# Two attention reads and a max-out layer: a bridge in DRAM, or one pass over the batches

## The chip, the cores and the metric

The kernel runs on one core of one Trainium2 chip. The metric is the device time of one execution in microseconds, taken as the median of several runs. A profile of one execution stands beside it; its clock runs from the first to the last instruction (the span). TensorE is PE in the profile, with its weight loads as PEld; VectorE is DVE, ScalarE is ACT, GpSimd is POOL, and SyncE, which only issues DMAs here, is SP.

## The reference

Eight batches, each with 8 heads, 512 tokens, 32 state rows and 64 values per head. Tokens read from the state and the state reads from the tokens; both results, 544 rows of 512 values per batch, go through a layer that takes the larger of two products.

```python
scores = scale * np.matmul(x, state.transpose(0, 1, 3, 2))
...
xread = np.matmul(a, state)
scores2 = scale * np.matmul(state, x.transpose(0, 1, 3, 2))
...
sread = np.matmul(a2, x)
return np.concatenate([xread, sread], axis=2).astype(np.float32)
...
h1 = x @ w1
h2 = x @ w2
g = np.maximum(h1, h2)
return (g @ w_out).astype(np.float32)
```

Here `a` and `a2` are softmaxes of the two score arrays. w1 and w2 are 512 x 1024, w_out is 1024 x 512, all in float32, as are x, state and the output of 4,352 rows (8 x 544).

## The kernel before, in words

Two stages stand one after the other, and a DRAM tensor `bridge` (512 x 4352, bf16) lies between them.

The attention stage loops over 8 batches and 8 heads. Per batch GpSimd's queue loads x and state with a cast to bf16 (L52, L57); x comes with tokens on partitions. Per head the kernel transposes the head's state (L61) and x (four transposes, L67) on TensorE, ScalarE copies them out of PSUM, four matmuls make the scores (L74), ScalarE takes the exponential (L78), VectorE sums, inverts and multiplies (L80, L83, L85). The normalised weights are transposed (L89), copied by ScalarE (L92) and multiplied by the state (L95, one matmul of 512 columns). VectorE casts the result (L97) and SP writes it to the bridge. The state's own read uses the same exponentials as weights (L106) and sums them with a column of ones (L108); the sums are turned by a transpose (L113), inverted (L117) and applied (L121), the result is transposed (L124) and written to the bridge too. Each kind of PSUM tile has one buffer, `p1` to `p8`. The order of the instructions of neighbouring heads is found by the framework's scheduler.

The MoE stage loads w1, w2 and w_out on GpSimd's queue (L144 to L148). Its tiles lie in memory that the first stage gives free, so that its first load waits for the last bridge write. Then it goes over 34 tiles of 128 rows: a load from the bridge (L155), eight slices of 128 hidden values with four matmuls for h1 (L164) and four for h2 (L167), a ScalarE cast of h1 to SBUF (L169) and a VectorE max with h2 (L170), then eight matmuls of 512 columns with w_out (L173), a VectorE copy (L176) and the store.

## Time and profile before

| What | us |
|---|---|
| Median of 3 runs | 427.98 (427.73 to 428.76) |
| Profiled execution, its span | 426.0 |
| TensorE busy | 376.9 (88%) |
| VectorE busy | 212.5 (50%) |
| ScalarE busy | 187.4 (44%) |
| GpSimd busy | 21.3 (5%) |
| Moved by DMA | 26.11 MB, mean 61 GB/s |

The profiled execution has no other time of its own than the span, which lies 2.0 us below the median of the runs. To read it: the busy shares are means over the two stages; the table by stage, the chain of waits and the timeline say which engine a stage waits for. Matmuls are pipelined, so the distance between the starts of two matmuls is their price, and the duration of one is longer.

### The profile page before, as it was taken

The numbers are of one execution on the slowest core, as the hardware profiler recorded it, in microseconds if no ns is written. First come the engines' busy times: TensorE is split into PE (matmuls) and PEld (weight loads), VectorE is DVE, ScalarE is ACT, GpSimd is POOL, SyncE is SP. The second block draws the span as 40 slices with busy tenths as digits, with TensorE's granted clock in tenths as the row PEclk, the third lists the DMA queues.
The fourth block names the chain that finished last, engine by engine and source line by source line (L and its number), as shares of the span: only waits on it lengthen the run. The fifth ranks groups of instructions, "written<-read, shape, count | busy, mean of one in ns | idle before, by whom it ended". The sixth has DMA issues, their size and how long they took to land.

```text
span 426.0 us, 10657 instructions
## 1 busy us (share of the span) xinstructions
PE 376.9 (88%) x3950; PEld 263.0 (62%) x3984; DVE 212.5 (50%) x755; ACT 187.4 (44%) x721; POOL 21.3 (5%) x25
## 2 busy tenths in 40 slices
PE   1999989999999999999860699999999999999996
PEld 1555555555455555555430578888888888888884
DVE  0455555554555545554540145555555555555553
ACT  1655555555555555555530233433433334333331
POOL 4002010020100201000002000000000000000000
PEclk9999999999999999999999999999999999999999
DMA  9209209091090911801016912222222222222211
GB/s 93 25 22 74 63 22 74 22 73 27 22 73 21 74 26 24 72 22 25 20 22 118 195 64 77 75 76 76 75 76 75 75 76 78 76 76 76 75 63 51
DMA packets 70307, 26.11 MB, mean 61 GB/s; under 512 B 59760, under 2 KB 64880, under 8 KB 70256
## 3 DMA queue, kind: packets, MB, share of 16 engines
q0 software_dynamic: 37168, 7.60, 20.7%
q1 hardware_dynamic: 33088, 17.84, 14.9%
q8 instruction: 31, 0.51, 0.5%
q14 instruction: 20, 0.16, 0.1%
HBM read 19.66 MB, written 13.37 MB: 78 GB/s over the span
## 4 chain that ended last, share of the span: by engine, by line
PE 79%; ACT 8%; DMA 6%; DVE 3%; issue 2%; POOL 0%; ACTq 0%; POOLq 0%; DVEq 0%
PE ph L167 14%; PE ph L164 14%; PE po L173 13%; PE p_xT L67 10%; PE p_xr L95 9%; ACT aT L92 8%; PE p_aT L89 8%; PE p_sr L106 5%; DMA wo<-in_moe_w_out_dram 4%; PE p_rs L113 2%; PE p_sT L61 2%; DMA x_bf<-in_x_dram 2%; PE p_rs L108 2%; DVE sr L121 1%; DMA bridge<-xr 0%
## 5 line engine op out<-in xcount | busy, mean ns | idle before, releaser
L169 ACT CAST gT<-ph 128x128 bf16<-128x128 f32 x272 | 72.3, 266 | 126.1 <-PE ph L164 126.0
L164 PE MATMUL ph<-xt,w 128*128 128x128 bf16 x1088 | 105.8, 221 | 12.2 <-DMA w<-in_moe_w_dram 12.1
L167 PE MATMUL ph<-xt,w 128*128 128x128 bf16 x1088 | 104.0, 219 | 1.8 <-DMA w<-in_moe_w_dram 1.8
L170 DVE TENSOR_TENSOR gT<-gT,ph 128x128 bf16<-128x128 bf16 x272 | 77.5, 287 | 52.9 <-ACT gT L169 31.5
L164 PEld LDWEIGHTS <-w 128*128 128x128 bf16 x1088 | 74.5, 99 | 21.4 <-issue 13.5
L167 PEld LDWEIGHTS <-w 128*128 128x128 bf16 x1088 | 72.7, 98 | 2.9 <-DMA w<-in_moe_w_dram 2.1
L67 PE MATMUL p_xT<-ident_bf,x_bf 128*64 128x128 bf16 x256 | 53.3, 315 | 9.3 <-DMA x_bf<-in_x_dram 8.7
L173 PE MATMUL po<-wo,gT 128*128 128x512 bf16 x238 | 57.1, 379 | 3.2 <-DMA wo<-in_moe_w_out_dram 1.5
L80 DVE TENSOR_REDUCE esum<-e_bf 128x4 f32<-128x128 bf16 x64 | 18.3, 285 | 80.0 <-ACT e_bf L78 80.0
L95 PE MATMUL p_xr<-aT,s_bf 32*64 32x512 bf16 x64 | 37.4, 584 | 13.2 <-ACT aT L92 13.2
L97 DVE CAST xr<-p_xr 64x512 bf16<-64x512 f32 x64 | 43.7, 683 | 9.9 <-PE p_xr L95 4.5
L176 DVE COPY ob<-po 128x512 f32<-128x512 f32 x34 | 23.5, 692 | 48.4 <-PE po L173 48.4
L106 PEld LDWEIGHTS <-e_bf 128*32 128x32 bf16 x256 | 21.8, 122 | 41.4 <-ACT e_bf L78 41.4
L92 ACT COPY aT<-p_aT 32x512 bf16<-32x512 bf16 x64 | 36.8, 575 | 23.6 <-PE p_aT L89 23.6
L173 PEld LDWEIGHTS <-gT 128*128 128x128 bf16 x272 | 25.2, 98 | 25.8 <-issue 1.6
L70 ACT COPY xT<-p_xT 64x512 bf16<-64x512 bf16 x64 | 36.2, 565 | 8.1 <-PE p_xT L67 8.0
L89 PE MATMUL p_aT<-ident_bf,a_bf 128*32 128x128 bf16 x256 | 38.9, 307 | 0.5 <-DVE a_bf L85 0.4
L67 PEld LDWEIGHTS <-x_bf 128*64 128x64 bf16 x256 | 23.7, 142 | 15.4 <-DMA x_bf<-in_x_dram 8.7
L63 ACT COPY sT<-p_sT 64x32 bf16<-64x32 bf16 x64 | 11.4, 179 | 44.4 <-PE p_sT L61 44.4
L106 PE MATMUL p_sr<-x_bf,e_bf 128*32 128x64 bf16 x256 | 30.4, 220 | 0.5 <-ACT e_bf L78 0.4
L108 PE MATMUL p_rs<-e_bf,ones_bf 128*1 128x32 bf16 x256 | 29.0, 213 | 0.0
L74 PE MATMUL p_sc<-sT,xT 64*128 64x32 bf16 x256 | 28.9, 193 | 0.0
(32 smaller groups left out, 269.9 us busy)
## 6 DMA issues: line engine op xcount, KB each, us to landing
out_dram<-ob SPq DMA_DIRECT2D x34, 256.0 KB, 2.0
xt<-bridge SPq DMA_DIRECT2D x34, 128.0 KB, 2.3
x_bf<-in_x_dram POOLq DMA_DIRECT2D x8, 512.0 KB, 7.7
bridge<-xr SPq DMA_DIRECT2D x64, 64.0 KB, 1.9
w<-in_moe_w_dram POOLq DMA_DIRECT2D x2, 1024.0 KB, 10.5
bridge<-srT SPq DMA_DIRECT2D x64, 4.0 KB, 1.6
wo<-in_moe_w_out_dram POOLq DMA_DIRECT2D x1, 1024.0 KB, 17.1
s_bf<-in_state_dram POOLq DMA_DIRECT2D x8, 32.0 KB, 5.3
```

The lines of the kernel that those rows point to most:

```text
L67: nc.tensor.matmul(p_xT[:, c, :], x_bf[:, h, c, :], ident_bf, is_transpose=True, start=(c == 0), stop=(c == NC - 1))
L89: nc.tensor.matmul(p_aT[:, c, :], a_bf[:, c, :], ident_bf, is_transpose=True, start=(c == 0), stop=(c == NC - 1))
L92: nc.scalar.copy(aT, p_aT)
L95: nc.tensor.matmul(p_xr, s_bf[:, h, :], aT.rearrange("n c p -> n (c p)"))
L97: nc.vector.tensor_copy(xr, p_xr)
L106: nc.tensor.matmul(p_sr, e_bf[:, c, :], x_bf[:, h, c, :], start=(c == 0), stop=(c == NC - 1))
L108: nc.tensor.matmul(p_rs, ones_bf, e_bf[:, c, :], start=(c == 0), stop=(c == NC - 1))
L164: nc.tensor.matmul(ph1[:, :mt], w1[:, k, f * 128:(f + 1) * 128], xt[:, k, :mt], start=(k == 0), stop=(k == n_k - 1))
L167: nc.tensor.matmul(ph2[:, :mt], w2[:, k, f * 128:(f + 1) * 128], xt[:, k, :mt], start=(k == 0), stop=(k == n_k - 1))
L169: nc.scalar.copy(gT[:, f, :mt], ph1[:, :mt])
L170: nc.vector.tensor_max(gT[:, f, :mt], gT[:, f, :mt], ph2[:, :mt])
L173: nc.tensor.matmul(po[:mt, :], gT[:, f, :mt], wo[:, f, :], start=(f == 0), stop=(f == n_kf - 1))
```

## The change

The kernel becomes one pass over the batches, and the bridge goes.

- Weights are combined on the chip. `wcat` holds Wc = w1 - w2 (1024 columns) and W2 Wo (512 columns). As max(h1, h2) = h2 + relu(h1 - h2), the output is relu(x (w1 - w2)) w_out + x (W2 Wo).
- The read of the state is folded into the layer. The 8 heads' state rows of a batch, multiplied by their part of `wcat`, make `SW` (2 x 128 pairs of head and state row, 1536 columns; `u_sw`, in three chunks of 512 columns, each eight matmuls of 64 x 32 weights). Layer 1 multiplies the attention weights `A` (transposed, `AT`) by `SW`.
- Attention works on all heads of a batch at once: x is loaded as float32 with 1 KB pieces, cast by GpSimd (batch 0 by VectorE and ScalarE), transposed 128 x 128; scores go against a block-diagonal state `sbd`; the sums for the state's read come from a column of ones in `xb`. GpSimd multiplies A by the inverse sums.
- The state's reads of all batches are kept in `sread_t` and pass the layer together in `moe_sread`, after batch 5.
- The order is written out by hand (`manual_schedule`). Three batches of attention (LEAD) run ahead, with the transposes of w2 (`w_t`) behind the first and W2 Wo (`w_wo`) behind the third. Then `moe(b)` has slots, after each of its eight layer-1 slices and four layer-2 tiles, filled with the attention of batch b+3 and `u_sw` of batch b+1. All PSUM tiles share eight buffers, taken in turn.

The diff, cut to the new functions (the removed lines are the kernel printed above, L35 to L177):

```diff
+    LEAD = 3
+    WC = FF + DM
...
+    psum = ctx.enter_context(tc.tile_pool(name="ps", bufs=8, space=bass.MemoryType.PSUM))
+    ctx.enter_context(tc.manual_schedule())
...
+    def load_x(b):
+        xf = xio.tile([128, H, NC * D], F32, tag="xf", name="xf")
+        xf_t[b] = xf
+        for g in range(2):
+            nc.sync.dma_start(
+                out=xf[:, 4 * g:4 * g + 4, :],
+                in_=x[b, 4 * g:4 * g + 4].rearrange("h (p c) d -> p h (c d)", c=NC),
             )
...
+    load_x(1)
+    load_x(2)
...
+    for wf, w in ((w2f, moe_w2), (w1f, moe_w1)):
+        for g in range(2):
             nc.sync.dma_start(
+                out=wf[64 * g:64 * g + 64],
+                in_=w[256 * g:256 * g + 256].rearrange("(i d) f -> d i f", i=4),
             )
...
+    def u_xt(b, half):
...
+        for cc in range(2):
+            c = 2 * half + cc
+            for k in range(4):
+                nc.tensor.transpose(p[:, (cc * 4 + k) * 128:(cc * 4 + k + 1) * 128],
+                                    d["xb"][:, c, k // 2, (k % 2) * 128:(k % 2) * 128 + 128], ident)
+        copy("A" if half else "V", d["xt"][:, 2 * half:2 * half + 2].rearrange("p c k t -> p (c k t)"), p)
...
+    def u_sc(b, half):
...
+        for cc in range(2):
+            for k in range(4):
+                nc.tensor.matmul(p[:, cc * 256 + k * 64:cc * 256 + k * 64 + 64],
+                                 d["xt"][:, 2 * half + cc, k, :], sbd[:, b, k, :],
+                                 start=(cc == 0 and k == 0), stop=(cc == 1 and k == 3))
...
+        nc.scalar.activation(out=d["e"][:, sl].rearrange("p c h n -> p (c h n)"), in_=p, func=ACTF.Exp, scale=scale)
+        nc.vector.tensor_reduce(d["es"][:, sl], d["e"][:, sl], axis=mybir.AxisListType.X, op=ALU.add)
+        nc.vector.reciprocal(d["er"][:, sl], d["es"][:, sl])
+        nc.gpsimd.tensor_mul(d["a"][:, sl], d["e"][:, sl],
+                             d["er"][:, sl].unsqueeze(3).to_broadcast([128, 2, H, Ns]))
...
+    def u_sr(b, g):
...
+        for c in range(NC):
+            nc.tensor.matmul(p[:, 0:257], d["e"][:, c, 4 * g:4 * g + 4, :].rearrange("p i n -> p (i n)"),
+                             d["xb"][:, c, g, 0:257], start=(c == 0), stop=(c == NC - 1))
...
+    def u_sw(b, ch):
...
+        pg = [bank(), bank()]
+        for i in range(4):
+            for g in range(2):
+                nc.tensor.matmul(pg[g][32 * i:32 * i + 32, :],
+                                 st2[64 * g:64 * g + 64, i, b * Ns:(b + 1) * Ns],
+                                 wcat[64 * g:64 * g + 64, i, ch * 512:(ch + 1) * 512],
+                                 start=True, stop=True)
+        for g in range(2):
+            copy("A" if g else "V", SW[b][:, g, ch * 512:(ch + 1) * 512], pg[g])
...
+    def moe(b, fill):
+        r = big.tile([128, NF, NC * 128], BF16, tag="r", name="r")
+        for f in range(NF):
+            p = bank()
+            for g in range(2):
+                nc.tensor.matmul(p, SW[b][:, g, f * 128:(f + 1) * 128], AT[b][:, g, :], start=(g == 0), stop=(g == 1))
+            relu(r[:, f, :], p)
+            for u in fill.get(f, ()):
+                u()
+        ob = big.tile([128, NC, DM], F32, tag="ob", name="ob")
+        for c in range(NC):
...
+            for g in range(2):
+                nc.tensor.matmul(p, AT[b][:, g, cs], SW[b][:, g, FF:WC], start=(g == 0), stop=False)
+            for f in range(NF):
+                nc.tensor.matmul(p, r[:, f, cs], wo[:, f, :], start=False, stop=(f == NF - 1))
+            copy("A" if c % 2 else "V", ob[:, c, :], p)
...
+    def w_t(i):
+        copy("A", w2b[:, i, :], w2f[:, i, :])
+        p = bank(BF16)
+        for f in range(NF):
+            nc.tensor.transpose(p[:, f * 128:(f + 1) * 128], w2b[:, i, f * 128:(f + 1) * 128], ident)
+        copy("V" if i % 2 else "A", w2t[:, i].rearrange("p f t -> p (f t)"), p)
...
+    for b in range(LEAD):
+        for u in att_units(b):
+            u()
+        if b == 0:
+            for i in range(4):
+                w_t(i)
+        if b + LEAD < B:
+            load_x(b + LEAD)
+    for i in range(4):
+        w_wo(i)
+    for i in range(4):
+        nc.vector.tensor_sub(wcat[:, i, 0:FF], w1f[:, i, :], w2f[:, i, :])
+    for ch in range(3):
+        u_sw(0, ch)
+
+    for b in range(B):
+        fill = {}
+        n = b + LEAD
+        if n < B:
+            cast_x(n)
+            u = att_units(n)
+            for slot, k in ((0, 0), (2, 1), (4, 2), (6, 3), (8, 4), (9, 5), (10, 6), (11, 7)):
+                fill.setdefault(slot, []).append(u[k])
+            if n + 1 < B:
+                fill.setdefault(1, []).append(lambda n=n: load_x(n + 1))
+        if b + 1 < B:
+            for slot, ch in ((3, 0), (7, 1), (9, 2)):
+                fill.setdefault(slot, []).append(lambda b=b, ch=ch: u_sw(b + 1, ch))
+        moe(b, fill)
+        if b == B - LEAD:
+            moe_sread()
```

Where the order of instructions matters to the prediction, it stands below as the two programs have it, first ScalarE's queue in the opening part. Before, ScalarE serves one head after another and has nothing to do with the weights:

```order
L70 COPY xT<-p_xT 64x512
L111 CAST rs_row<-p_rs 1x32
L119 COPY sr_raw<-p_sr 32x64
L63 COPY sT<-p_sT 64x32
L92 COPY aT<-p_aT 32x512
L126 COPY srT<-p_srT 64x32
L78 ACTIVATE e_bf<-p_sc 128x128
```

With the change, ScalarE's queue from its cast of batch 0 on (`w2f` and `w2b` are W2 as loaded and in bf16, `w2t` is its transpose, `sread_t` the state's read; L58 is the helper `copy`):

```order
L58 CAST xb<-xf 128x4x4x64 [waits DMAHW3_49]
L58 COPY sbd<-ps 64x16x32 [waits DVE_49] x2
L58 COPY xt<-ps 128x1024 [waits PE_49]
L165 ACTIVATE e<-ps 128x512 [waits PE_49] x2
L58 COPY sread_t<-ps 128x4x32 [waits PE_49]
L58 CAST w2b<-w2f 128x1024 [waits DMAHW7_49,DMAHW5_49]
L58 COPY w2t<-ps 128x1024 [waits PE_49]
L58 CAST w2b<-w2f 128x1024 x2
L58 COPY w2t<-ps 128x1024 [waits PE_49]
L58 CAST w2b<-w2f 128x1024
L58 COPY xt<-ps 128x1024 [waits PE_49]
```

The work on W2, which waits for its load, now stands between attention 0 and attention 1, whose copy of xt is the last row.

The second place is VectorE's queue in the main work. Before, one head in the attention stage:

```order
L80 TENSOR_REDUCE esum<-e_bf 128x4
L97 CAST xr<-p_xr 64x512
L83 RECIPROCAL resum<-esum 128x4
L115 CAST rs_col<-p_rs_1839 32x1
L85 TENSOR_TENSOR a_bf<-e_bf,resum 128x128
L117 RECIPROCAL rrs<-rs_col 32x1
L121 TENSOR_SCALAR sr<-sr_raw,rrs 32x64
```

With the change, `moe(0)` from its first slot through layer 1 to the first store copy (`r` is the relu, `sw` is S Wc of the next batch, `es` and `er` the sums of batch 3's exponentials and their inverses):

```order
L60 COPY xt<-ps 128x1024 [waits PE_49]
L228 TENSOR_SCALAR r<-ps 128x512 [waits PE_49] x2
L60 CAST sw<-ps 128x512 [waits PE_49]
L166 TENSOR_REDUCE es<-e 128x16 [waits Activation_49]
L167 RECIPROCAL er<-es 128x16 [waits DVE_49,Pool_49]
L228 TENSOR_SCALAR r<-ps 128x512 [waits PE_49]
L166 TENSOR_REDUCE es<-e 128x16 [waits Activation_49]
L167 RECIPROCAL er<-es 128x16 [waits DVE_49]
L228 TENSOR_SCALAR r<-ps 128x512 [waits PE_49]
L60 CAST sw<-ps 128x512 [waits PE_49]
L60 COPY ob<-ps 128x512 [waits PE_49]
```

Attention's reduces, which wait for ScalarE, stand between the relus that layer 2 reads.

## Rows read from the trace of the kernel before

**Rows 1.** The page: span and busy time of each engine.

```profile
span 426.0 us, 10657 instructions
PE 376.9 (88%) x3950; PEld 263.0 (62%) x3984; DVE 212.5 (50%) x755; ACT 187.4 (44%) x721; POOL 21.3 (5%) x25
```

**Rows 2.** By stage: stretch, length; busy PE, PEld, DVE, ACT, POOL; clock; DMA; GB/s.

```profile
120.00:180.00 60.00, 55.46 (x437) 31.90 (x437) 32.62 (x128) 32.48 (x128) 4.54 (x4) 1.00 0.44 45
300.00:400.00 100.00, 99.00 (x1342) 82.43 (x1359) 54.92 (x171) 40.45 (x152) 0.00 (x0) 1.00 0.25 76
...
234.60:244.70 10.10, 6.89 (x76) 5.71 (x77) 2.05 (x8) 2.67 (x10) 0.00 (x0) 1.00 1.12 195
```

**Rows 3.** The chain that ended last, in order of time: start, length, work.

```profile
1.29 7.39 DMA x_bf<-in_x_dram
...
223.27 1.92 DMA bridge<-xr
...
250.22 1.67 PE po L173 x7
255.54 1.67 PE po L173 x7
...
422.13 0.69 DVE ob L176
```

**Rows 4.** Timeline, TensorE in one head of the attention stage: start, length, instruction.

```profile
100.54 0.23 PE L106 MATMUL p_sr<-x_bf,e_bf 128*32 128x64 bf16 x1
...
100.83 0.21 PE L108 MATMUL p_rs<-e_bf,ones_bf 128*1 128x32 bf16 x1
100.97 0.42 PE L67 MATMUL p_xT<-ident_bf,x_bf 128*64 128x128 bf16 x2
...
101.98 0.61 PE L89 MATMUL p_aT<-ident_bf,a_bf 128*32 128x128 bf16 x4
102.52 0.26 PE L74 MATMUL p_sc<-sT,xT 64*128 64x32 bf16 x3
...
103.81 0.23 PE L106 MATMUL p_sr<-x_bf,e_bf 128*32 128x64 bf16 x1
```

**Rows 5.** Groups by line and shape: busy us, mean ns, idle before.

```profile
L173 PE MATMUL po<-wo,gT 128*128 128x512 bf16 x238 | 57.1, 379 | 3.2 <-DMA wo<-in_moe_w_out_dram 1.5
...
L97 DVE CAST xr<-p_xr 64x512 bf16<-64x512 f32 x64 | 43.7, 683 | 9.9 <-PE p_xr L95 4.5
...
L92 ACT COPY aT<-p_aT 32x512 bf16<-32x512 bf16 x64 | 36.8, 575 | 23.6 <-PE p_aT L89 23.6
...
L176 DVE COPY ob<-po 128x512 f32<-128x512 f32 x34 | 23.5, 692 | 48.4 <-PE po L173 48.4
...
L121 DVE TENSOR_SCALAR sr<-sr_raw,rrs 32x64 bf16<-32x64 f32 x64 | 20.1, 314 | 7.2 <-ACT sT L63 0.5
L80 DVE TENSOR_REDUCE esum<-e_bf 128x4 f32<-128x128 bf16 x64 | 18.3, 285 | 80.0 <-ACT e_bf L78 80.0
...
L78 ACT ACTIVATE e_bf<-p_sc 128x128 bf16<-128x128 f32 x64 | 17.0, 266 | 1.2 <-PE p_sc L74 1.1
...
L83 DVE RECIPROCAL resum<-esum 128x4 f32<-128x4 f32 x64 | 10.2, 160 | 0.1
```

**Rows 6.** Timeline, TensorE as the three weights arrive, one after the other.

```profile
234.61 3.34 PE L164 MATMUL ph<-xt,w 128*128 128x128 bf16 x27 [12.09 <-DMA w<-in_moe_w_dram]
...
239.75 0.62 PE L167 MATMUL ph<-xt,w 128*128 128x128 bf16 x8 [1.80 <-DMA w<-in_moe_w_dram]
...
244.76 1.89 PE L173 MATMUL po<-wo,gT 128*128 128x512 bf16 x7 [1.46 <-DMA wo<-in_moe_w_out_dram]
```

**Rows 7.** Groups of GpSimd: its one elementwise row and a memset of one element.

```profile
masks.py:199 POOL TENSOR_SCALAR_AFFINE_SELECT ident_bf<-ident_bf 128x128 bf16<-128x128 bf16 x1 | 0.3, 311 | 0.1
...
L192 POOL MEMSET const-bfloat16-1.0<- 128x1 bf16 x1 | 0.1, 102 | 0.0
```

More of the change, by code (lines that the diff above doesn't have):

```diff
@@ L133 @@
[L133 to L154 removed]
+    stage = ctx.enter_context(tc.tile_pool(name="stage", bufs=1))
@@ L155 @@
+    load_x(0)
+    s_f = stage.tile([128, B // 4, DM], F32)
+    for b in range(B):
+        nc.scalar.dma_start(
+            out=s_f[32 * (b % 4):32 * (b % 4) + 32, b // 4, :].rearrange("n (h d) -> n h d", h=H),
+            in_=state[b].rearrange("h n d -> n h d"),
+        )
+    load_x(1)
+    load_x(2)
+    w2f = stage.tile([128, 4, FF], F32)
+    w1f = stage.tile([128, 4, FF], F32)
+    for wf, w in ((w2f, moe_w2), (w1f, moe_w1)):
+        for g in range(2):
             nc.sync.dma_start(
-                out=xt[:, :, :mt],
@@ L171 @@
-            po = ps.tile([M_TILE, d_model], F32, tag="po")
-            for f in range(n_kf):
-                nc.tensor.matmul(po[:mt, :], gT[:, f, :mt], wo[:, f, :],
-                                 start=(f == 0), stop=(f == n_kf - 1))
-            ob = sb.tile([M_TILE, d_model], F32, tag="ob")
-            nc.vector.tensor_copy(ob[:mt], po[:mt])
-            nc.sync.dma_start(out=out[m0:m1, :], in_=ob[:mt])
+                out=wf[64 * g:64 * g + 64],
+                in_=w[256 * g:256 * g + 256].rearrange("(i d) f -> d i f", i=4),
+            )
@@ new lines, in moe_sread @@
+    def moe_sread():
+        NT = B * Ns
+        r = big.tile([128, NF, NT], BF16, tag="rs", bufs=1, name="rs")
+        for f in range(NF):
+            p = bank()
+            for i in range(4):
+                nc.tensor.matmul(p[:, 0:NT], wcat[:, i, f * 128:(f + 1) * 128], sread_t[:, i, :],
+                                 start=(i == 0), stop=(i == 3))
+            relu(r[:, f, :], p[:, 0:NT])
+        ob = big.tile([128, NT // 128, DM], F32, tag="obs", bufs=1, name="obs")
+        for t in range(NT // 128):
+            p = bank()
+            ts = slice(t * 128, (t + 1) * 128)
+            for i in range(4):
+                nc.tensor.matmul(p, sread_t[:, i, ts], wcat[:, i, FF:WC], start=(i == 0), stop=False)
+            for f in range(NF):
+                nc.tensor.matmul(p, r[:, f, ts], wo[:, f, :], start=False, stop=(f == NF - 1))
+            copy("A" if t % 2 else "V", ob[:, t, :], p)
+            for q in range(4):
+                b = 4 * t + q
+                nc.sync.dma_start(out=out[b * L + S:(b + 1) * L], in_=ob[32 * q:32 * q + 32, t, :])
@@ new lines, in w_t, with w_wo @@
+    def w_t(i):
+        copy("A", w2b[:, i, :], w2f[:, i, :])
+        p = bank(BF16)
+        for f in range(NF):
+            nc.tensor.transpose(p[:, f * 128:(f + 1) * 128], w2b[:, i, f * 128:(f + 1) * 128], ident)
+        copy("V" if i % 2 else "A", w2t[:, i].rearrange("p f t -> p (f t)"), p)
+    def w_wo(i):
+        p = bank()
+        for f in range(NF):
+            nc.tensor.matmul(p, w2t[:, i, f, :], wo[:, f, :], start=(f == 0), stop=(f == NF - 1))
+        copy("A", wcat[:, i, FF:WC], p)
@@ new lines @@
+    for ch in range(3):
+        u_sw(0, ch)
+    for b in range(B):
+        fill = {}
[13 more added lines that the diff above has]
+            moe_sread()
```

242 lines of the change are left out of this document (122 added, 120 removed).

## The prediction

> **What bounds the kernel now.** I read the page's busy line first, then the table by stage, then the chain of waits, and last the timeline inside one head and one token tile. The busy line [rows 1] says TensorE: 376.9 of 426.0 us, against 212.5 for VectorE and 187.4 for ScalarE. The table by stage [rows 2] shows that this is true twice, for different reasons. In the attention stage (120 to 180 us) TensorE is busy 55.46 of 60 us; in the MoE stage (300 to 400 us) 99.0 of 100. The chain [rows 3] gives the shape: first load to 8.7 us, 64 heads until the last bridge write is issued at 223.3, then a wait for the weights, then 34 token tiles, each 5.32 us after the one before (250.22, 255.54), and from the start of the last output copy at 422.13 to the end of the span 3.9 us.
>
> The two stages do not run at the same pace. In one head [rows 4] four pairs of matmuls with 64 and 32 columns start from 100.54 to 100.83: 352 columns in 0.29 us, 1.21 columns per ns. [...] In the MoE stage seven 512-column matmuls take 1.67 us [rows 3] where one alone is 379 ns [rows 5]: (1.67 - 0.379)/6 = 0.215 us each, 2.4 GHz. A tile of 5.32 us less 8 x 0.215 leaves 3.60 us for 64 matmuls of 128 columns, 0.056 us each. So 128 columns cost 0.106 us in the attention stage and 0.056 in the MoE stage. A head is 3.27 us (100.54 to 103.81), 64 of them 209 us; 34 tiles are 181 us. Between them, 223.3 to 234.6 us [rows 3, 6], TensorE has nothing to do. [...]
>
> **What the change does to the columns.** Before, a tile of 128 tokens streams 64 x 128 + 8 x 512 = 12,288 columns, 34 tiles 417,792. After, one batch of 512 tokens streams 16 x 512 in layer 1 (contraction over 256 pairs of head and state row, and no second product) and 40 x 512 in layer 2 (32 for the relu, 8 for the linear part): 56 matmuls x 0.215 = 12.05 us. Eight batches are 96.4 us. The state rows add 32 matmuls of 256 columns and 24 of 512: 32 x 0.109 + 24 x 0.215 = 8.6 us. W2 Wo adds 32 of 512: 6.9 us.
>
> Attention per batch has 28 transposes, 16 score matmuls of 64 columns and 8 read matmuls of 257. Between the dense matmuls of the main loop I price it at 2.4 GHz: 28 x 0.056 + 16 x 0.045 (between half of 0.056 and 0.056) + 8 x 0.108 = 3.15 us. In the opening part, where it waits on copies, at 1.21 columns per ns: 2.97 + 0.85 + 1.70 = 5.5 us.
>
> **S Wc.** This is the disputed price: 24 chunks (three per batch), each eight matmuls of 64 x 32 weights and 512 columns. The eight read disjoint strips of rows and write disjoint partitions. No row of before shows two strips at once; the pairs in [rows 4] use one strip and add up. So a chunk lies between 0.215 us (all eight side by side) and 1.72 (one after the other). To either come two changes of array shape: from 100.83 to 100.97 [rows 4] 0.14 us pass where 32 columns explain 0.03, and four transposes take 0.54 where 4 x 0.106 = 0.42, so 0.11 to 0.12 us a change. The ends are 0.45 and 1.95. I take 0.5, because nothing that one of the eight reads or writes belongs to another, unlike the pairs in the row. [...]
>
> **Main loop.** Five batches carry the next attention and the next S Wc: 12.05 + 3.15 + 1.5 = 16.7 us. Do the other engines cover? For 512 columns out of PSUM ScalarE needs 0.575 us and VectorE 0.69 [rows 5]. The slopes against the 128-column rows are (575 - 266)/384 = 0.80 ns and (683 - 285)/384 = 1.04 ns per column, so 1,024 columns are 0.99 and 1.22 us. ScalarE per batch: 11 x 0.575 + 0.99 + 0.27 = 7.6 us. VectorE: 9 copies, relus and casts x 0.69 + 2 x 1.22 + 2 reduces x 0.68 + 2 reciprocals x 0.16 + 2 x (0.16 + 0.51) for the sread (314 ns for 64 columns, 192 more) = 11.7 us. Both below 16.7. Within layer 1 it is closer: VectorE has 7.1 us of work there and TensorE about 6, and two reduces that wait for ScalarE's exp stand ahead of the relus of f=5 and f=7 on VectorE's queue. I followed that queue: the relu of f=7 is ready about 0.4 us after layer 2's first tile wants it. So 17.1 us. GpSimd's 2 x 1,024 + 2 x 512 elements, by its only elementwise row (311 ns for 128, with 102 fixed [rows 7]: 1.63 ns per element), take 5.4 us a batch and are hidden unless they cost over three times that. The x loads and the 1 MB stores, together 2 MB per 17 us, need 0.12 MB/us where the transfers of [rows 2] ran at 0.195, so they are covered; on SP's queue a load stands behind the store of the batch before, but a whole batch ahead of its use.
> Sum: 5 x 17.1 + 2 x 13.55 + 12.05 + 8.6 = 133.3 us.
>
> **Opening part.** Nothing of MoE can start until S Wc of batch 0, and TensorE's order puts the four W2 transposes (w_t) behind attention 0 and ahead of attention 1, so the landing of w2f holds everything. Ahead of or beside it are x 0 to 2 (3.1 MB), state (0.5), w2f and wo (2.1 each): 7.9 MB. The weight loads of before land 5.1 us apart (234.61, 239.75, 244.76 [rows 6]) for 2.1 MB read and 1.05 MB written as bf16: 0.41 MB/us read, 0.2 written. At 0.39 that is 20 us, plus the start at 1.3 [rows 3], plus 3.5 for state, whose 256-byte pieces go like the first x load (1 MB in 7.4 us): 25 us. Ends: 16 (wo does not compete) and 42 (the float32 that is now written counts, 7.9/0.195). Then:
> - w_t: ScalarE casts four times 1,024 columns and copies twice between, 6 x 0.99, with two waits of 0.86 for eight transposes: 7.7 us.
> - attention 1 and 2, in order and with nothing between: transposes 0.84, copy 1.22, scores 0.45, two exps 1.15, reduce, reciprocal and GpSimd product 0.68 + 0.16 + 0.94, A's transposes 0.84, sread's 0.42, and half a microsecond of handovers: 7.2 us each, 14.4.
> - W2 Wo 6.9 and its last cast 0.6. The four VectorE subtractions of 1,024 columns (about 1.2 us each) run beside it if w1f has landed.
> - S Wc 0: 3 x 0.5 + 0.7.
> Sum 25 + 7.7 + 14.4 + 7.5 + 2.2 = 56.8 us. In place of 223 us before the bridge is full, and of the 11.3 us weight wait, which goes; late instead is w2f.
> W2 and w1 are fetched in halves of 64 partitions. [...]
>
> **Sum.** 56.8 + 133.3 + 3.9 [rows 3] for the end = 194.0 us of span, against 426.0. The median of the runs, 427.98, is 2.0 above that span; **196 us**.
>
> **The rivals.**
> - S Wc one after the other: 24 x (1.95 - 0.5) = 35 us more, 231. For it: the row's pairs add up. Against: disjoint strips. Chance 0.12. [...]
> - Loads late, because float32 written to the chip moves at the 0.195 MB/us of [rows 2]: w2f at 42, 213 us. For it: that stretch had every DMA engine full (share 1.12). Against: it was converting. Chance 0.14.
> - VectorE becomes the bound: if its PSUM reads cost twice my rows, 23 us a batch against 17.1, five times 6: 226 us. Against: nine of its nineteen instructions have a row of the same size. Chance 0.06.
> - [...] Chance 0.03.
> - Slower than before: GpSimd. It now casts x and multiplies A, in order: 14 casts of 1,024, 16 products and 2 state casts of 512, 23,552 elements that every u_xt and u_at waits for. With some 40 us that it does not cover, the total passes 426 from (426 - 40)/23,552 = 16.4 ns per element, ten times [rows 7]. That row is one short instruction, which is why I don't exclude it. Chance 0.02, at 430 or more.
>
> **How the numbers follow.** My case has 0.63. Its own range is 177 (wo out of the way: -9; attention at 6 us; no 0.4 stalls; S Wc at 0.45) to about 214. The loads rival and VectorE as the bound lie below 226; S Wc in a row, the slow clock and GpSimd lie beyond, 0.17 together, with a little below 177. So 177 to 226. A measurement of this kernel tells about 0.3% from no change. Only the GpSimd case is slower: faster 0.975, same 0.005, slower 0.02.
>
> **What would show it.** Right: in the timeline, S Wc's eight matmuls start within some 0.3 us; layer 2's 512-column matmuls stand 0.215 us apart; batches 0 to 4 take about 17 us each between the first layer-1 matmuls, the last about 12; the first W2 transposes wait for w2f near 25 us and the first layer-1 matmul starts near 57. The busy line should have TensorE's share lower than before and GpSimd at 45 us. Wrong: eight matmuls of a chunk 0.2 us apart, 512 columns at 0.43 us, TensorE idle behind VectorE or GpSimd in the main loop, or a first layer-1 matmul after 75 us.

## The result, and the profile after

The changed kernel took 202.12 us (median of 4 runs, 201.42 to 204.53) against 428.18 us for the kernel before (median of 4 runs on the same chip, 427.73 to 428.76). The ratio is 0.4714, 95% interval [0.4702, 0.4726]. The forecast was 196.0 us with a range of 177 to 226: faster, as said, inside the range, and 6.1 us too low. The profiled execution took 202.35 us for a span of 200.5 us, 1.85 us around it where I had put 2.0. Medians here are over all runs of a kernel, while the ratios leave out runs more than 1.5% above a kernel's fastest, and three of the profiles are of such a run (the state's loads issued first, the first kernel without side-by-side tiles, and the state on SyncE's queue).

The page of the changed kernel: span and busy time of each engine, to be held against [rows 1].

```profile
span 200.5 us, 2915 instructions
...
PE 160.0 (80%) x1192; PEld 83.1 (41%) x1192; DVE 92.3 (46%) x171; ACT 70.6 (35%) x123; POOL 34.3 (17%) x47
```

TensorE's busy time went from 376.9 to 160.0 us and its share from 88 to 80%. Most of the missing fifth lies at the front: 34.7 of the 40.5 us without a matmul fall before 64.4 us. The table by stage shows it; its columns are those of [rows 2].

```profile
0.00:24.00 24.00, 1.97 (x17) 1.45 (x18) 3.56 (x7) 2.91 (x3) 3.00 (x10) 1.00 0.97 247
32.20:41.20 9.00, 3.84 (x32) 3.15 (x33) 0.75 (x2) 5.86 (x7) 0.00 (x0) 0.50 1.16 242
41.20:56.20 15.00, 10.16 (x107) 7.62 (x106) 8.39 (x21) 4.48 (x7) 4.74 (x6) 0.81 0.66 216
56.20:64.40 8.20, 8.13 (x59) 3.38 (x56) 6.56 (x7) 3.12 (x7) 1.38 (x2) 1.00 0.01 2
64.40:148.60 84.20, 82.71 (x661) 41.58 (x662) 49.76 (x97) 35.17 (x66) 18.52 (x22) 1.00 0.27 88
```

From 64.4 us on, TensorE is busy 82.71 of 84.20 us, and VectorE, ScalarE and GpSimd 49.76, 35.17 and 18.52: the main loop is TensorE's, as forecast. In the first 24 us it does 1.97 us of work while the DMA engines are full (share 0.97, 247 GB/s), and from 32.2 to 41.2 us it waits for ScalarE at a granted clock of 0.50.

The chain of waits, in order of time (start, length, work), answers to [rows 3]:

```profile
10.04 12.45 DMA s_f<-in_state_dram
...
74.14 1.73 PE ps L246 x8
...
90.86 1.73 PE ps L246 x8
```

Layer 2's second tile of batches 0 and 1 starts 16.72 us apart (74.14 and 90.86), and the chain is TensorE almost throughout. Ahead of that stands what I had not in my sum: the last of the eight state loads is issued at 10.04 and lands at 22.49. The timeline shows what it holds, and then each stage of the opening (VectorE, TensorE and ScalarE lines, put in order of time):

```profile
10.14 0.43 DVE L60 CAST s_bf<-s_f 128x512 bf16<-128x512 f32 x1 [4.40 <-DMA s_f<-in_state_dram]
22.62 0.43 DVE L60 CAST s_bf<-s_f 128x512 bf16<-128x512 f32 x1 [10.45 <-DMA s_f<-in_state_dram]
23.98 1.91 PE L147 MATMUL ps<-ident,xb 128*128 128x128 bf16 x16
32.16 1.05 ACT L58 CAST w2b<-w2f 128x1024 bf16<-128x1024 f32 x1
41.20 1.91 PE L147 MATMUL ps<-ident,xb 128*128 128x128 bf16 x16
...
56.19 7.07 PE L290 MATMUL ps<-wo,w2t 128*128 128x512 bf16 x32
63.19 1.13 PE L213 MATMUL ps<-wcat,st 64*32 64x512 bf16 x24
64.44 0.60 PE L235 MATMUL ps<-aT,sw 128*128 128x512 bf16 x2
...
66.64 0.59 PE L235 MATMUL ps<-aT,sw 128*128 128x512 bf16 x2
67.17 0.41 PE L213 MATMUL ps<-wcat,st 64*32 64x512 bf16 x8
67.51 0.60 PE L235 MATMUL ps<-aT,sw 128*128 128x512 bf16 x2
...
72.88 0.39 PE L246 MATMUL ps<-wo,r 128*128 128x512 bf16 x1 [0.61 <-DVE r L228]
...
89.59 0.39 PE L246 MATMUL ps<-wo,r 128*128 128x512 bf16 x1 [0.21 <-DVE r L228]
```

`states(1)`, the state of batches 4 to 7, stands in TensorE's order ahead of attention 0 (L147 at 23.98), though attention 0 needs only that of batches 0 to 3, which was there at 10.14. So attention 0 ran to 31.95 instead of beside the landing of w2f, and w_t began at 32.16 with no wait for w2f at all. The lines from 66.64 to 67.51 carry the disputed price: eight matmuls of one S Wc chunk are over in 0.41 us, and the next matmul starts 0.34 us after the first of them. With the change of shape ahead of it the chunk costs 0.44 us, as the two matmuls at 66.64 take 0.43 (2 x 0.215) and the next of their kind starts 0.87 after them. The last two lines are the last matmul of layer 2's first tile in batches 0 and 1, waiting for the relu of f=7.

The groups that the prediction sized from [rows 5, 7] (busy us, mean ns, idle before):

```profile
L246 PE MATMUL ps<-wo,r 128*128 128x512 bf16 x256 | 61.3, 379 | 1.4 <-DVE r L228 1.4
L228 DVE TENSOR_SCALAR r<-ps 128x512 bf16<-128x512 f32 x32 | 21.4, 670 | 11.0 <-PE ps L235 10.9
L62 POOL CAST xb<-xf 128x1024 bf16<-128x1024 f32 x14 | 14.2, 1042 | 0.0
L58 ACT COPY xt<-ps 128x1024 bf16<-128x1024 bf16 x8 | 8.1, 1009 | 5.3 <-PE ps L147 4.0 <-DVE xt L60 1.3
L60 DVE COPY xt<-ps 128x1024 bf16<-128x1024 bf16 x8 | 5.5, 692 | 10.9 <-PE ps L147 10.9
```

512 columns cost VectorE 670 ns, as priced; 1,024 bf16 columns cost it 692 and not the 1,220 that my slope gave, while ScalarE's 1,009 are on its slope. GpSimd's cast of 1,024 is 1,042 ns, where 1.63 ns per element gave 1,670. Layer 2 waited 1.4 us in all for a relu: 0.61 in batch 0 and 0.21 in each of the four after it.

### The profile page after: what moved, and what is told of

Its sections match the earlier page's. It is cut to its first block, busy times and chain, and to the rows that moved or that the text cites. A ratio compares the mean times of both kernels' runs of the same rounds, so it can differ in the third digit from the quotient of the medians.

```text
span 200.5 us, 2915 instructions
## 1 busy us (share of the span) xinstructions
PE 160.0 (80%) x1192; PEld 83.1 (41%) x1192; DVE 92.3 (46%) x171; ACT 70.6 (35%) x123; POOL 34.3 (17%) x47
## 4 chain that ended last, share of the span: by engine, by line
PE 61%; DMA 10%; DVE 9%; ACT 9%; POOL 6%; issue 3%; ACTq 1%; DVEq 0%; POOLq 0%
PE ps L246 24%; DMA s_f<-in_state_dram 10%; PE ps L235 9%; PE ps L244 6%; DVE es L166 4%; PE ps L290 3%; PE ps L147 3%; DVE r L228 3%; PE ps L213 3%; POOL a L168 3%; PE ps L178 2%; PE ps L189 2%; ACT e L165 2%; PE ps L284 2%; ACT xt L58 2%
## 5 line engine op out<-in xcount | busy, mean ns | idle before, releaser
L246 PE MATMUL ps<-wo,r 128*128 128x512 bf16 x256 | 61.3, 379 | 1.4 <-DVE r L228 1.4
L246 PEld LDWEIGHTS <-r 128*128 128x128 bf16 x256 | 25.0, 98 | 33.5 <-DVE r L228 3.9
L235 PE MATMUL ps<-aT,sw 128*128 128x512 bf16 x128 | 33.4, 380 | 0.1
L58 ACT COPY ob<-ps 128x512 f32<-128x512 f32 x16 | 9.4, 586 | 67.5 <-PE ps L246 67.5
L168 POOL TENSOR_TENSOR a<-e,er 128x512 bf16<-128x512 bf16 x16 | 16.6, 1048 | 85.1 <-DVE er L167 71.6
L228 DVE TENSOR_SCALAR r<-ps 128x512 bf16<-128x512 f32 x32 | 21.4, 670 | 11.0 <-PE ps L235 10.9
L226 ACT ACTIVATE r<-ps 128x512 bf16<-128x512 f32 x32 | 19.4, 607 | 4.8 <-PE ps L235 4.8
L244 PE MATMUL ps<-sw,aT 128*128 128x512 bf16 x64 | 19.2, 381 | 0.0
L60 DVE CAST sw<-ps 128x512 bf16<-128x512 f32 x24 | 16.2, 680 | 5.2 <-PE ps L213 5.2
L58 ACT CAST sw<-ps 128x512 bf16<-128x512 f32 x24 | 13.9, 591 | 2.2 <-PE ps L213 2.2
L62 POOL CAST xb<-xf 128x1024 bf16<-128x1024 f32 x14 | 14.2, 1042 | 0.0
L147 PE MATMUL ps<-ident,xb 128*128 128x128 bf16 x128 | 11.7, 252 | 0.0
L147 PEld LDWEIGHTS <-xb 128*128 128x128 bf16 x128 | 10.5, 117 | 2.4
L58 ACT COPY xt<-ps 128x1024 bf16<-128x1024 bf16 x8 | 8.1, 1009 | 5.3 <-PE ps L147 4.0
```

What stands on the lines that cost most here:

```text
L58: nc.scalar.copy(o, i)
L60: nc.vector.tensor_copy(o, i)
L62: nc.gpsimd.tensor_copy(o, i)
L147: nc.tensor.transpose(p[:, (cc * 4 + k) * 128:(cc * 4 + k + 1) * 128], d["xb"][:, c, k // 2, (k % 2) * 128:(k % 2) * 128 + 128], ident)
L168: nc.gpsimd.tensor_mul(d["a"][:, sl], d["e"][:, sl], d["er"][:, sl].unsqueeze(3).to_broadcast([128, 2, H, Ns]))
L226: nc.scalar.activation(out=o, in_=p, func=ACTF.Relu)
```

## The experiments

Two questions were open: whether the S Wc price was right for the reason given, and what set the opening. The first two runs ask about state, the next two about S Wc, one about W2 Wo, and the rest try to give the opening back. The last ratio of a paragraph is always to the kernel before.

### The state's second half, moved behind w_t

```diff
     states(0)
-    states(1)
...
         if b == 0:
             for i in range(4):
                 w_t(i)
+            states(1)
```

Expected:

> Edit: the preparation of the state rows of batches 4 to 7 (states(1)) moves from ahead of attention 0 to behind the W2 transposes; nothing else. Theory A: attention 0 began at 24.0 us because TensorE's order has states(1) ahead of it, and the second half of state lands only at 22.5; so attention 0 now begins near 13 (after ScalarE's last state DMA issue at 10.4, its table load and the cast of x), ends near 21, the W2 transposes then wait for w2f near 22 to 25, and the first layer-1 matmul moves from 64.4 to about 56: span 192, time 194. Rival B: the opening is bound by all of the loads together, so w2f comes later than 30 us and the time stays at 201 to 202.

Measured: 200.84 us (198.34 to 202.73), ratio 0.4656 [0.4621, 0.4691]. Attention 0 ran from 12.66 to 20.4, and w_t then waited for w2f, as the prediction had it for the change itself. Yet only 1.3 us came of it. The timeline of this kernel (ScalarE, then TensorE) and one stretch by stage:

```profile
25.86 1.04 ACT L58 CAST w2b<-w2f 128x1024 bf16<-128x1024 f32 x1 [5.16 <-DMA w2f<-in_moe_w_dram]
...
37.05 1.91 PE L147 MATMUL ps<-ident,xb 128*128 128x128 bf16 x16
...
52.70 9.00 PE L290 MATMUL ps<-wo,w2t 128*128 128x512 bf16 x32
...
62.88 0.61 PE L235 MATMUL ps<-aT,sw 128*128 128x512 bf16 x2
```

```profile
52.70:56.00 3.30, 3.30 (x10) 1.22 (x9) 3.30 (x4) 0.27 (x1) 0.91 (x1) 0.50 0.02 5
```

w_t starts 6.3 us sooner (25.86 against 32.16). Then most of it is given back: w_t and the moved `states(1)` take 11.2 us to the start of attention 1 (37.05) where w_t alone took 9.0, attentions 1 and 2 take 15.65 against 14.99, and W2 Wo takes 9.00 against 7.07 us. That last loss goes with the clock: for the first 3.3 us of W2 Wo the granted clock was 0.50, and ten matmuls started, where the change has 1.00 throughout (56.20 to 64.40 above). The first layer-1 matmul is at 62.88 instead of 64.44. So the wait for the state was real, and without it w_t starts 6.3 us sooner, of which this execution keeps 1.5. That the 1.9 us at W2 Wo belong to the edit is not shown: the kernel with two strips of rows below has the change's own order on TensorE up to there, and took 8.77.

### The state's loads issued ahead of x 0

The eight issues were moved ahead of `load_x(0)` in the program, still on ScalarE's queue.

> Edit: the eight state loads are issued before the load of x 0 instead of after; the order of TensorE stays. Theory A: the state's second half was late because its last four loads each wait for an earlier DMA before they are issued and then stand behind 3 MB of x and 2 MB of w2f; issued first, all of state lands by about 6 us, attention 0 begins at 10 to 13, and the gain is that of the run with states(1) moved or somewhat more: time 192 to 195. Rival B (the loads together are the bound): no change, 201 to 202. Rival C (state's 256-byte pieces are slow in themselves): state's second half still lands after 15 us and the gain is under 5 us.

Measured: 201.27 us (199.11 to 204.19), ratio 0.4655 [0.4641, 0.4669], 1.3% under the change's. The second half still landed at 20.36, 2.1 us sooner than in the change. That has the signs of Rival C, but the edit did not make the order it was meant to make, so none of the three was tested. x goes out on another queue (SyncE's), so the order of the two in the program says nothing about who goes first; ScalarE's eight issues lasted to 10 us either way.

### S Wc without side-by-side tiles

Two kernels. In the first the 64 x 32 weights of S Wc are set into 128 x 128 ones filled with zeros, so that the eight matmuls of a chunk use the whole array one after the other. In the second they become 64 x 128, so that the two row halves may still run side by side, but not the four column strips. In both GpSimd places the weights, which is added work.

```diff
-                nc.tensor.matmul(pg[g][32 * i:32 * i + 32, :],
-                                 st2[64 * g:64 * g + 64, i, b * Ns:(b + 1) * Ns],
-                                 wcat[64 * g:64 * g + 64, i, ch * 512:(ch + 1) * 512],
-                                 start=True, stop=True)
+                nc.tensor.matmul(pg[g], stw[b % 2][0:128, g, i, :],
+                                 wcat[0:128, i, ch * 512:(ch + 1) * 512],
+                                 start=(i == 0), stop=(i == 3))
```

The second has `64 * g:64 * g + 64` in place of both `0:128`. Expected of the first and of the second:

> Edit: S Wc with weights padded by zeros to 128 rows and 128 columns, so that the eight matmuls of a chunk use the whole array one after the other; same result, eight small GpSimd copies per batch added. If the strips side by side are what made the chunk 0.44 us, a chunk costs 8 x 0.215 = 1.72 us without a change of array shape: 24 x 1.28 = 31 us more, time 233. If something else set the chunk (its two copies out of PSUM), the time stays within 3 us of 202.

> Edit: as the unpacked run, but with weights of 64 rows and 128 columns: two strips of rows, no strips of columns. If strips of rows run side by side as such, a chunk is 4 x 0.215 plus two changes of shape of 0.12 = 1.1 us: 24 x 0.65 = 16 us more, time 218. If only strips of columns ran side by side, a chunk is 1.72 + 0.24: 36 us more, time 238.

Measured: 230.48 us (2 runs, 227.92 and 233.05) and 218.61 us (2 runs, 217.60 and 219.62; ratio 0.5099 [0.5071, 0.5127]). One chunk and the layer-1 block behind it, from TensorE's timeline of the first kernel and then of the second:

```profile
73.19 1.89 PE L216 MATMUL ps<-wcat,stw 128*128 128x512 bf16 x8
74.91 0.59 PE L244 MATMUL ps<-aT,sw 128*128 128x512 bf16 x2
```

```profile
59.35 8.77 PE L299 MATMUL ps<-wo,w2t 128*128 128x512 bf16 x32
...
73.48 1.04 PE L216 MATMUL ps<-wcat,stw 64*128 64x512 bf16 x8
74.44 0.61 PE L244 MATMUL ps<-aT,sw 128*128 128x512 bf16 x2
```

A chunk holds TensorE for 1.72 us in a row, 0.96 us in two strips of rows and 0.34 us in the change (67.17 to 67.51 above). With the changes of shape these are 1.72, 1.06 and 0.44. Times 24 chunks the first is 31 us more than the change and the second 15; the kernels are some 26 to 31 (its two runs) and 16.5 us slower. The 31 is the profiled run; why the other took 5 us less is open. The price of 0.5 us was right, and it was right because the eight run side by side: in the change one of them lasts 386 ns (median), and all eight are over in 0.41 us. Both kernels keep TensorE's order of the change up to S Wc, and W2 Wo took 7.07 us in the first, as in the change, and 8.77 in the second (59.35 above), at a granted clock of 0.53 in 59.6 to 63 us.

### W2 Wo not multiplied out

Layer 1 makes both products and takes their maximum; layer 2 loses its linear part; w_t, w_wo and the subtraction go.

```diff
-            relu(r[:, f, :], p)
+            q = bank()
+            for g in range(2):
+                nc.tensor.matmul(q, SW[b][:, g, FF + f * 128:FF + (f + 1) * 128], AT[b][:, g, :], start=(g == 0), stop=(g == 1))
+            copy("A", r[:, f, :], p)
+            nc.vector.tensor_max(r[:, f, :], r[:, f, :], q)
```

> Undoes one part: W2 Wo is not multiplied out. Layer 1 makes both products (S W1 and S W2, four chunks of S Wc), ScalarE evicts one and VectorE takes the maximum with the other, layer 2 loses its linear part, and the stages w_t (9.0 us) and w_wo (7.0) with the difference W1-W2 are gone. Theory A (the multiplied-out part costs all of its opening time on the path, and saves 8 matmuls of 512 columns in each batch and one chunk): first layer-1 matmul about 48.5 instead of 64.4, main loop 8 x (8 x 0.216 + 0.44) = 17.3 longer, sread 1.8 longer: 202.1 - 16 + 19 = 205. Rival B (the opening is set by weight loads anyway, so that taking out the two stages gains little): first layer-1 matmul at 58 or later, time 215 to 221. Rival C (VectorE becomes the bound: 8 two-input maxima of 512 columns in each batch in place of 4 relus): batch spacing 21 us or more against 18.9 by A, time over 222.

Measured: 209.28 us (207.84 to 209.77), ratio 0.4877 [0.4858, 0.4895]. Theory A had 205, with the first layer-1 matmul at 48.5. From the timeline and the chain:

```profile
46.94 3.88 ACT L58 CAST wcat<-w1f 128x1024 bf16<-128x1024 f32 x4
...
52.69 0.93 PE L233 MATMUL ps<-aT,sw 128*128 128x512 bf16 x2
```

```profile
62.24 1.90 PE ps L246 x8
...
80.81 1.89 PE ps L246 x8
```

Batches are 18.57 us apart (62.24 to 80.81), against 18.9 forecast and 16.72 in the change, so VectorE's maxima are no bound. The opening gained 11.75 us, not 16: ScalarE casts W1 in a row behind attention 2 (3.88 us), which I had left out. So multiplying W2 Wo out costs about 12 us in front and buys 17 behind (from the first layer-1 matmul to the last matmul 148.8 us here and 131.9 in the change): 5.3 us between the two profiled spans, 7.2 between the medians.

### The state on SyncE's queue

```diff
-    load_x(0)
...
-        nc.scalar.dma_start(
+        nc.sync.dma_start(
             out=s_f[32 * (b % 4):32 * (b % 4) + 32, b // 4, :].rearrange("n (h d) -> n h d", h=H),
...
+    load_x(0)
```

> The eight state loads are issued from SyncE's queue ahead of x 0, everything else as in the changed kernel. Theory A (states(1), which stands ahead of attention 0 in TensorE's order, waits for the state's second half only because that half's loads come behind x on the rings): state all landed by 7, attention 0 runs from about 10.5 to 18.3 instead of 23.98 to 31.95, w_t then waits for w2f (about 25), first layer-1 matmul at 58 to 61 instead of 64.4, time 197 to 199 (with 2 us less of gain if W2 Wo runs at a low clock as it did where the states were moved). Rival B (the gain is given back whole by x 0 and w2f, which land later behind the state): attention 0 begins at 15 or later, w2f at 28 or later, time 201 to 203.

Measured: 206.48 us (205.02 to 208.96), ratio 0.4806 [0.4786, 0.4826]: 4.4 us slower than the change, which neither theory had. The state was there at 6.4, so its 256-byte pieces are not slow in themselves, which was Rival C when the issues were moved ahead of x 0. Attention 0 began at 12.27, and then (GpSimd, TensorE and ScalarE in the timeline):

```profile
6.95 1.06 POOL L297 DMA_DIRECT2D wo<-in_moe_w_out_dram  x1
...
27.29 1.04 POOL L62 CAST xb<-xf 128x1024 bf16<-128x1024 f32 x1 [2.86 <-DMA xf<-in_x_dram]
...
29.40 0.39 PE L189 MATMUL ps<-ident,a 128*128 128x128 bf16 x2 [11.34 <-POOL a L168]
...
36.66 1.05 ACT L58 CAST w2b<-w2f 128x1024 bf16<-128x1024 f32 x1 [4.70 <-DMA w2f<-in_moe_w_dram]
```

Two waits took the place of the one removed. On GpSimd's queue the casts of x 1 and x 2 stand ahead of attention 0's products, so these wait until x 2 is there (27.29). And GpSimd, no longer held by the state, issues the load of W_out at 6.95 instead of 23.47; it now shares the DMA engines (share 1.07, 247 GB/s from 7 to 37 us) with W2, which lands at 36.66 instead of before 24.8.

### The opening in another order

From here on several things change at once, and their shares are not separated. State first on SyncE's queue; batch 0 cast by VectorE alone; the units of attentions 0 to 2 interleaved ahead of w_t; x 2's cast behind them on GpSimd's queue; W2 cast by VectorE and copied by ScalarE; one of four subtractions on GpSimd; x 4 and x 5 loaded once instead of twice (the change loads them in the opening and again from the slots).

> Opening put in another order, main loop as in the changed kernel: state first on SyncE's queue, attention 0 to 2 interleaved unit by unit ahead of w_t (so that a unit of one batch runs while another's waits for VectorE or GpSimd), W2 cast on VectorE and its copies on ScalarE, one of the four subtractions on GpSimd, and x 4 and x 5 loaded once, not twice. Theory A (the opening is lost to attentions that run one behind the other and to waits for loads, and its work is about 2 x 7.2 + 7.7 + 7.5 + 1.3 = 31 us behind the first attention): first layer-1 matmul at 44 to 48, time 181 to 186. Rival B (loads bound the opening: some 10 MB ahead of w2f and w1f at about 250 GB/s): first layer-1 matmul at 50 to 54, time 187 to 192. Rival C (W2 Wo at the low clock, twice its 7.0 us): first layer-1 matmul beyond 54, time over 192.

Measured: 191.28 us (189.2 to 193.14), ratio 0.4429 [0.441, 0.4448]. Rival B: the loads. The chain of this kernel in the opening:

```profile
12.30 30.00 DMA w1f<-in_moe_w_dram
42.40 6.50 DVE wcat L313 x3
```

Layer 2's first tile stands in TensorE's timeline:

```profile
57.48 1.67 PE L246 MATMUL ps<-wo,r 128*128 128x512 bf16 x7
```

All three attentions are done by 31 us, beside the loads; W1 lands at 42.4 and the first layer-1 matmul is at 50.2. VectorE's three subtractions took 6.5 us, where the four of the changed kernel took 5.28 in a row, the shortest of them 1.21. While GpSimd made the fourth (42.43 to 45.83, 3.40 us), the one that began at 42.40 took 1.22 and the one that began at 43.54 took 3.37: it ended at 46.91, 1.08 us after GpSimd's. Why the second took so long no run here shows.

### Weights on a second queue, and two batches ahead instead of three

Both start from the last kernel and also make W1 - W2 in column halves on VectorE alone. The first issues W2 and W1 from ScalarE's queue at the start. The second keeps them on SyncE's and sets `LEAD = 2`, with x 2 behind the weights.

> From the reordered opening (191.28 us, first layer-1 matmul at 50.20, bound by w1f's landing at 42.4 and 6.5 us of subtractions). Two edits: W1 and W2 are issued from ScalarE's queue at the start, beside the state and x on SyncE's, so that the first 15 us, which moved 128 to 214 GB/s at a DMA share of about 0.55, carry weights too; and W1-W2 is made in column halves on VectorE alone, so that layer 1 starts behind half of it. Theory A (the opening is issue-bound at first and byte-bound after, some 8.5 MB in all; the two halves add): w1f landed by 36 to 38, first layer-1 matmul at 42 to 45 (no sooner, W2 Wo and the attentions being ahead of it on TensorE), time 183 to 186. Rival B (the rate with weights in it stays at about 240 GB/s whatever the queue, and x and state come later for it): w1f at 40 to 43, first layer-1 matmul at 45 to 48, time 186 to 189, all of it from the subtractions. Rival C (state and x 0 are held back by the weights beside them, as the state was behind x in the changed kernel): attention 0 begins at 20 or later, first layer-1 matmul at 50 or later, time 191 or more.

> From the same reordered opening, weights left on SyncE's queue; the column halves as well, and two batches of attention ahead of the main loop, not three: x 2 is loaded behind the weights, and its attention runs among the blocks of batch 0. Theory A (bytes ahead of w1f bind: 1 MB less at 240 GB/s is 4.2 us, the halves 2.6 to 4; one more batch of the main loop carries an attention, 16.7 - 13.4 = 3.3 us): first layer-1 matmul at 42 to 44, main loop 3.3 longer, time 186 to 188. Rival B (TensorE's order binds, W2 Wo at the low clock 8 to 9 us behind w2f's landing): first layer-1 matmul at 45 to 47, time 189 to 192.

Measured: 204.22 us (203.63 to 204.81; ratio 0.4754 [0.4739, 0.4769]) and 190.84 us (189.86 to 191.88; ratio 0.4447 [0.4427, 0.4467]). From VectorE's timeline of the first and TensorE's of the second:

```profile
29.54 0.69 DVE L60 CAST xb<-xf 128x1024 bf16<-128x1024 f32 x1 [11.26 <-DMA xf<-in_x_dram]
```

```profile
36.92 0.58 PE L289 MATMUL ps<-wo,w2t 128*128 128x512 bf16 x1 [7.23 <-DMA wo<-in_moe_w_out_dram]
37.73 9.11 PE L289 MATMUL ps<-wo,w2t 128*128 128x512 bf16 x30 [0.22 <-issue]
```

In the first, Rival C: x 0 was complete at 29.5 (9.8 in the reordered opening), held back by weights that nothing needed yet. In the second W2 was there at 26.5, but now W_out came last: TensorE waited 7.23 us for it and then ran W2 Wo from 36.92 to 46.84. The first layer-1 matmul is at 48.0, and the time is that of the reordered opening within the spread, near Rival B's forecast but with another wait.

### Subtraction in column halves, and the partition halves on two queues

Both start from the reordered opening.

```diff
-    for i in range(4):
-        (nc.gpsimd if i == 3 else nc.vector).tensor_sub(wcat[:, i, 0:FF], w1f[:, i, :], w2f[:, i, :])
-    for ch in range(3):
-        u_sw(0, ch)
+    for h in range(2):
+        hs = slice(512 * h, 512 * h + 512)
+        for i in range(4):
+            nc.vector.tensor_sub(wcat[:, i, hs], w1f[:, i, hs], w2f[:, i, hs])
+        if h == 0:
+            u_sw(0, 0)
...
+        if b == 0:
+            fill.setdefault(1, []).append(lambda: u_sw(0, 1))
+            fill.setdefault(5, []).append(lambda: u_sw(0, 2))
```

> From the reordered opening (191.28 us): W1-W2 is made in column halves, all four of each on VectorE, and the second and third chunk of S Wc go among the first blocks of layer 1. Theory A (behind w1f's landing at 42.4 the path is only VectorE's three subtractions, which took 2217 ns each beside GpSimd's one and 1298 alone in the changed kernel; four half-width ones are 2.6): first layer-1 matmul at 45.5 to 47 instead of 50.2, time 186 to 188. Rival B (TensorE is still in W2 Wo at the low clock when the half is ready, or the second half's subtractions hold layer 1 again at its fifth block): first layer-1 matmul at 46 to 47 but the first layer-2 block comes less than 2 us sooner than in the reordered opening (60.6), time 189 to 192.

> The same as e11_sub_halves, and the two partition halves of W2 and of W1 go out on two queues side by side (SyncE's and, behind x 0's cast, ScalarE's) instead of one behind the other. Theory A (the 215 to 250 GB/s of the stretch in which the weights land is the rate of one half of the partitions; both at once reach the 300 to 370 of the x stretches): w2f landed by 27 to 29 instead of 32.7, w1f by 36 to 38 instead of 42.4, first layer-1 matmul 2 to 5 sooner than in e11_sub_halves (W2 Wo then being the wait), time 182 to 185. Rival B (the rate is set by something else, such as the load of W_out that is cast on its way, and does not know halves): w1f landed at 41 to 44, GB/s of the 20 to 40 us stretch still 215 to 250, time within 2 us of e11_sub_halves.

Measured: halves alone 187.80 us (187.35 to 190.83), ratio 0.4370 [0.436, 0.438], the best of this study, 7% under the changed kernel (0.4370 / 0.4714 = 0.927). The first layer-2 tile in TensorE's timeline:

```profile
56.74 1.89 PE L246 MATMUL ps<-wo,r 128*128 128x512 bf16 x8
```

The time is Theory A's, but the trace has Rival B's sign. The first layer-1 matmul is at 45.99, 4.2 us sooner than in the reordered opening, and the first layer-2 tile only 0.7 us sooner (56.74 against 57.48): the rest goes to waits among the first blocks. The 60.6 of the expectation is the reordered opening's second tile, and its 1,298 ns are of the kernel with the state on SyncE's queue; the changed kernel's four subtractions took 1,376 on average. With the halves on two queues as well, and the copies of the state's preparation all on VectorE, it is 195.89 us (195.18 to 199.61), ratio 0.4561 [0.4546, 0.4577]. By stage, first the kernel with one queue, then that with two:

```profile
30.00:40.00 10.00, 7.50 (x58) 5.13 (x59) 4.95 (x11) 4.71 (x6) 1.54 (x3) 0.83 1.02 217
40.00:50.00 10.00, 8.24 (x49) 3.23 (x47) 7.25 (x11) 3.05 (x6) 2.22 (x2) 0.88 1.06 318
```

```profile
15.00:30.00 15.00, 4.13 (x64) 3.10 (x62) 5.62 (x14) 4.03 (x7) 3.27 (x5) 0.72 1.10 263
30.00:40.00 10.00, 6.51 (x58) 5.58 (x58) 4.11 (x10) 2.36 (x4) 4.13 (x5) 0.56 1.03 214
```

Halves of W2 and then W1 on the one queue moved at 217 GB/s (30 to 40 us), and the next x loads, which fill all partitions, at 318 (40 to 50, W1's last 2.3 us included). With two queues the stretch in which both halves are under way, with x and W_out, has 263 (15 to 30 us), 21% more than 217. ScalarE's half of W1 landed at 29.4, SyncE's at 41.9, and once the one queue is left the rate is 214. So the stretch with both moved more than either stretch with one, but less than that of the x loads, and the second queue pulled weights ahead of x 1, for whose cast TensorE waited until 33.2 us. How much of the 21% is the pairing, and how much x and W_out, was not separated. Nor do the runs tell whether the partitions or the 4 KB pieces of the weights set the 214 to 217.

### Batch 0's first slots

In the best kernel TensorE stood for some 2.5 us among the first blocks, for x 3 and for the second half of W1 - W2. The attention units 0 to 2 and the second chunk were moved behind blocks 3 to 5.

> From e11_sub_halves (187.8 us, first layer-1 matmul at 45.99, first layer-2 block at 56.74). Only the order of TensorE's work among the first blocks of batch 0 is changed: attention 3's first three units and the second chunk of S Wc stand behind layer-1 blocks 3 to 5 in place of 0, 1, 2 and 4, so that blocks 1 to 3, which need neither x 3 nor the second half of W1-W2, run while these come. Theory A (TensorE stood for about 2.5 us there, 0.78 of it for the cast of x 3 and the rest for the second half's subtractions): first layer-2 block at 54 to 55.5, time 185.5 to 187. Rival B (the waits only move behind block 3, since the second half is ready at the same 48.5 and the chunk's copies and attention 3 still stand ahead of layer 2): first layer-2 block at 56 or later, time 187.5 to 188.5.

Measured: 189.09 us (188.75 to 189.80), ratio 0.4415 [0.4408, 0.4422]; the first layer-2 tile is at 57.34. From TensorE's timeline:

```profile
47.78 1.90 PE L235 MATMUL ps<-aT,sw 128*128 128x512 bf16 x8 [0.77 <-DVE sw L60]
...
52.58 0.60 PE L235 MATMUL ps<-aT,sw 128*128 128x512 bf16 x2 [1.79 <-DVE sw L60]
```

Blocks 0 to 3 now run in a row, and the wait stands behind them (1.79 us): Rival B, though the time is 0.6 us above its range and 1.3 above the best kernel. The 0.6 us that the first layer-2 tile is later is no more than W1's landing, 0.9 us later in this execution (43.2 against 42.3), and the two profiled spans differ by no more than that (186.5 and 185.9); the rest of the 1.3 is not located.

## Why the prediction was right, and where it missed

**What bounds it, and the main loop: right.** TensorE sets the loop, 82.71 of 84.20 us. The 2.4 GHz of the forecast is its name for 512 columns in 0.215 us, 2.38 a ns; no run shows a frequency, only that pace and a granted clock of 1.00 beside it, and none shows why the heads of before went at 1.21 a ns under the same 1.00. Batches came 16.72 us apart where 17.1 was forecast, those without attention 13.4 (13.55), the state rows 8.7 (8.6), the last batch 12.2 (12.05): 131.9 us against 133.3. The end took 4.2 instead of 3.9. The late relu came where I had put it, at the last matmul of layer 2's first tile, but at 0.21 us in four batches of five (0.61 in batch 0) where I had 0.4. VectorE had less to do than I had put down: 49.76 us in 84.2, 9.95 a batch instead of 11.7, the 1,024-column copies being 0.69 and not 1.22 us. The slope behind the 1.22 was drawn between unlike rows: its upper point is a float32 cast out of PSUM, its lower one (285 ns) a sum of bf16 numbers in SBUF, and these tiles are bf16 in PSUM.

**S Wc: right, with its reason shown.** 0.44 us a chunk with its shape changes against 0.5, which was my estimate and had no run behind it; the two kernels that take the side-by-side run away cost 26 to 31 and 16.5 us.

**The opening: 64.4 us against 56.8, and the term that failed is the first.** The prediction said that "the landing of w2f holds everything". It did not. W2 had landed by 24.8 us (its second half issued at 11.01, at most 13.8 to landing), as forecast, and nobody was waiting for it: attention 0 stood ahead, held to 23.98 by `states(1)`, whose loads landed at 22.5. I had counted state's bytes (3.5 us) but not who waits for them in TensorE's order. That puts w_t at 32.16 instead of 25: 7.2 of the opening's miss of 7.6. Of the rest, w_t took 9.04 (7.7 forecast), attentions 1 and 2 14.99 (14.4), W2 Wo 7.0 with its cast hidden (7.5) and S Wc 1.25 (2.2): +1.3, +0.6, -0.5, -0.9.

Moving that wait away gave 1.3 us and not 7, so that edit alone did not bring the time to the forecast. Behind each wait in this opening stands another, on another queue: w2f, then GpSimd's casts of x, then W_out, then W1.

**The 25 us for w2f was luck, right by errors that cancel.** I divided 7.9 MB by 0.39 MB/us and added 3.5 us for the state. The stretch ran at 247 GB/s, and W_out's 2.1 MB were not in it: GpSimd issued them at 23.47, behind the state's casts on its queue. 5.8 MB at 0.247 is 23.5 us, from 1.3. At the 217 GB/s that halves reached in a later run, W2 alone is 9.7 us (an estimate), against 5.4 for its 2.1 MB at the forecast's 0.39 MB/us. Where W_out did go out at 7 us, W2 landed at 36.7 (state on SyncE's queue) and 32.7 (reordered opening). Two ends were also added up wrongly: 16 and 42 us for w2f leave out those 3.5, and the range's lower end of 177 comes to 181 from the savings it names (9 + 2.4 + 2 + 1.2).

**The rivals.** S Wc in a row would have been 228 to 233; the forecast gave 231. VectorE, GpSimd (34.3 us busy in all where I had 45, 1,042 ns for 1,024 elements) and the slow clock, to which the forecast gave 0.03, did not come: the main loop ran at a granted clock of 1.00 (64.4 to 148.6 us). In the opening it fell to 0.50, in 32.2 to 41.2 us. Loads late did not come as written either (w2f at 42): what came late was the state, in loads of 64 KB.
